# First mixture, state tokens: the tokens as loaded operand in both layers, summed in rows, turned once at the end

## The chip, the cores and the metric

One core of a Trainium2 chip runs the whole program. Its engines work beside each other, each through its own queue in order: TensorE (PE) multiplies 128x128 tiles into PSUM, VectorE (DVE), ScalarE (ACT) and GpSimd (POOL) work on vectors, and SyncE (SP) issues DMAs. A matmul instruction has two operands: one, of 128 columns, is loaded into the array ahead of it (a weight load, PEld in the profile), the other is streamed through it, with up to 512 columns. The metric is the device time of one execution in microseconds.

## The reference, cut to what matters

Attention between 4 x 512 tokens and 4 x 32 state tokens gives 2304 tokens of 512 features. A first mixture layer with a leaky activation follows, then a second mixture of 8 experts with a balanced gate.

```python
def _moe_ref(x, w_in, w_out, alpha):
    h = x @ w_in
    g = np.maximum(h, 0.0) + alpha * np.minimum(h, 0.0)
    return (g @ w_out).astype(np.float32)

def _moe2_ref(x, w_gate, w1, w2):
...
    for e in range(E):
        h = np.maximum(x @ w1[e], 0.0)
        ye = h @ w2[e]
        out += P[:, e:e + 1] * ye
```

In the first mixture `x` is 2304x512, `w_in` 512x2048 and `w_out` 2048x512. `P` comes from `exp` of the logits `x @ w_gate`, scaled eight times over its rows and columns.

## The kernel before

Matmuls are done in three terms: every operand is split into a high part and the rest of it (`wh_t`, `wl_t`; `xs[0]`, `xs[1]`; `gh`, `gl`), and low x high, high x high and high x low are summed in PSUM.

The first mixture goes through its 2048 hidden columns in 8 **units** `u` of `FU` = 256, each of `NF` = 2 halves `f` of 128. A unit has five **chunks** of tokens `c`: four of 512 tokens, and the last one, `c == CS`, the 128 **state tokens** (4 x 32). For a chunk there are two jobs: `layer1(u, c, f)` makes the hidden columns of half `f` and their activation, `layer2_first(u, c, d)` multiplies them by the unit's rows of `w_out` and gives one block `d` of 128 output features, which is added to `acc`. Everywhere the features stand in the partitions and the tokens in the columns, so that the weights are the loaded operand and the tokens are streamed: 512 columns for a normal chunk, 128 for the state chunk. (For normal chunks layer 1 has been rewritten: it streams attention weights against `v`, a product of state tokens and weights that `make_v` prepares for every unit in four pieces, each 6 matmuls of 256 columns, `pv`.)

The state chunk's layer 1 takes 4 feature tiles x 3 terms = 12 matmuls for each half, 24 in all; its layer 2 takes 2 halves x 3 terms for each of 4 blocks, again 24. All four blocks stand side by side in one PSUM bank and are added to `acc` at once.

After layer 1 come three steps: ACT takes the negative part out of PSUM (`r`, L527), DVE completes the leaky activation (`leak`, L530), ACT and POOL split it (`halves`, L535 and L536). They are not written down at once but put into a list `soon` with a number of **slots** to wait; `slot()` (L1236) is called after every half of layer 1 and every block of layer 2, runs what is due, and lets background work go one step: the lane `w` converts the next unit's weights from their loaded form (`to_f32`, L109 to L123: a chain over DVE, ACT, POOL and again DVE) and splits them (L138, L139), the lane `v` makes `v`, and near the end lanes make the experts' forms (L626 to L635) and the gate. So the number of slots decides where background work stands among the matmuls.

The jobs follow `order` (L1203): `program` puts layer 1 of the next chunk before layer 2 of the one before, so the state chunk's layer 2 comes after layer 1 of the next unit's chunk 0. Up to the first job of unit 2 a scheduler may reorder the instructions; from there on each engine runs them as written (`manual_schedule`). PSUM pools: `ps_h` (3 banks) for layer 1, `ps_o` (3) for layer 2, `ps_a` (2) for `pv`, transposes and the gate.

Of the kernel before, what the change touches and what calls it, by code (L numbers as in the profile page):

```python
# [8 lines left out]
F32 = mybir.dt.float32  # L9
# [35 lines left out]
def body(ctx: ExitStack, tc: tile.TileContext, xt_in, xn_in, stb, stk, wd, ws, alpha, wgate, out):  # L45
# [82 lines left out]
    def split_w(u, j):  # L128
# [8 lines left out]
        src = src_t[u, j]  # L137
        nc.scalar.activation(out=wh_t[u, j], in_=src, func=AF.Copy)  # L138
        nc.gpsimd.tensor_tensor(out=wl_t[u, j], in0=src, in1=f32(wh_t[u, j]), op=ALU.subtract)  # L139

    def w1(t, u, k, f):
        return t[u, f][:, k * P:(k + 1) * P]

    def w2(t, u, f, c0, n):
        return t[u, NF + f][:, c0:c0 + n]
# [355 lines left out]

    v_done = set()

    def layer1(u, c, f):
        n = S if c < CS else NS_ALL
        if f == 0:
            g_t[u, c] = (
                gp.tile([P, NF, S], F32R, tag="gh", name=f"gh{u}_{c}"),
                gp.tile([P, NF, S], F32R, tag="gl", name=f"gl{u}_{c}"),
            )  # L510
        gh, gl = g_t[u, c]
        ps = ps_h.tile([P, 512], F32, tag="h", name=f"ph{u}_{c}_{f}")[:, :n]
        if c < CS:
            vh, vl = (v_of(u, c)[i][:, :, f * P:(f + 1) * P] for i in range(2))
            terms = [(w[:, k, :], x[:, k, :]) for k in range(2) for w, x in ((vh, al[c]), (vh, ah[c]), (vl, ah[c]))]
        else:
            terms = [
                (w1(wt, u, k, f), x[:, k, :])
                for k in range(KD) for wt, x in ((wh_t, xs[1]), (wh_t, xs[0]), (wl_t, xs[0]))
            ]  # L520
        for i, (w, x) in enumerate(terms):
            nc.tensor.matmul(ps, lhsT=w, rhs=x, start=(i == 0), stop=(i == len(terms) - 1))  # L522
        hi, lo = gh[:, f, :n], gl[:, f, :n]
        fa = u * NF + f
        r = tp.tile([P, S], F32, tag="r", name=f"r{u}_{c}_{f}", bufs=3)[:, :n]

        nc.scalar.activation(out=r, in_=ps, func=AF.Relu, scale=-1.0)  # L527

        def leak():
            nc.vector.scalar_tensor_tensor(  # L530
                out=r, in0=r, scalar=beta[:, fa:fa + 1], in1=ps, op0=ALU.mult, op1=ALU.add
            )

        def halves():
            nc.scalar.activation(out=hi, in_=r, func=AF.Copy)  # L535
            nc.gpsimd.tensor_tensor(out=lo, in0=r, in1=f32(hi), op=ALU.subtract)  # L536

        soon.append([1, leak])
        soon.append([2, halves])

    def layer2_first(u, c, d):

        n = S if c < CS else NS_ALL
        gh, gl = g_t[u, c]
        if c < CS or d == 0:
            po_t[c < CS] = ps_o.tile([P, 512], F32, tag="o", name=f"po{u}_{c}_{d}")
        ps = po_t[c < CS][:, :n] if c < CS else po_t[False][:, d * n:(d + 1) * n]
        i = 0
        for f in range(NF):
            for wt, g in ((wh_t, gl), (wh_t, gh), (wl_t, gh)):  # L550
                nc.tensor.matmul(  # L551
                    ps, lhsT=w2(wt, u, f, d * P, P), rhs=g[:, f, :n], start=(i == 0), stop=(i == 3 * NF - 1)
                )
                i += 1
        bank = po_t[c < CS]

        def evict():
            for g, there, here in places(c):
                if g not in acc:
                    new_acc(g)  # L560
                if c < CS:
                    a, src = acc[g][:, d, there], bank[:, here]
                else:
                    a, src = acc[g][:, :, there], bank.rearrange("p (d n) -> p d n", d=KD)
                if u == 0:
                    nc.scalar.activation(out=a, in_=src, func=AF.Copy)
                else:
                    nc.vector.tensor_tensor(out=a, in0=src, in1=a, op=ALU.add)  # L568

        if c < CS or d == KD - 1:  # L570
            soon.insert(0, [1, evict])

    po_t = {}

# [659 lines left out]
    def slot():  # L1236
        tick()
        for lane in lanes:
            if wait[lane] > 0:
                wait[lane] -= 1  # L1240
            else:
                advance(lane)
# [96 lines left out]
    def run(program):  # L1339
        for kind, u, c in program:  # L1340
            if kind == 1:

                while done["a"] < min(c, B - 1):
                    advance("x")
                if c == CS:
                    states_to(B - 1)
                while (u, 1) not in split:
                    advance("w")
                while c < CS and u == 1 and done["scores"] < 2 + c // 2:
                    advance("x")  # L1350
                while c < CS and (u, c // 2) not in v_done:
                    advance("v")
                if (u, c) == (1, 2):
                    lanes["w"].append(convert(2, range(2)))
                if (u, c) == (2, 0):
                    nc.scalar.activation(out=wg[:, :, :E], in_=wg_raw, func=AF.Copy)
                    nc.vector.tensor_tensor(out=wg[:, :, E:], in0=wg_raw, in1=f32(wg[:, :, :E]), op=ALU.subtract)
                if (u, c) == (U1 - 1, 0):
                    while (u, NPIECE - 1) not in split:
                        advance("w")  # L1360
                    load_a(0, rawp)
                    lanes["w"].append(weights_a(0))
                if c == 0 and 2 <= u < U1 - 1:
                    lanes["w"].append(weights(u + 1, 0, 0 if u == U1 - 2 else 1))
                    lanes["v"].append(make_v(u + 1))
                for f in range(NF):
                    layer1(u, c, f)
                    slot()
                if (u, c) == (0, CS):

                    lanes["w"].append(weights(2, 2, 0))
                    lanes["v"].append(make_v(2))
            else:
                while (u, NPIECE - 1) not in split:
                    advance("w")
                if (u, c) == (0, 1):

                    states_to(1)
                    while (1, 2) not in split:
                        advance("w")  # L1380
                for i in range(KD):
                    layer2_first(u, c, i)
                    slot()
                if u == U1 - 1:

                    if c == 0:
                        made.update(forms(0))
                    forms_in(made, ("B11", "T1 T3 T2", "", "", "")[c])
                    if c == 2:
                        lanes["gate"].append(gate())  # L1390
                if u == U1 - 2 and c == 3:
                    forms_in(made, "B22")
                if (u, c) == (U1 - 1, CS):
                    forms_in(made, "B21 T4")
# [138 lines left out]
```

## Time and profile before

| | us |
|---|---|
| median of 3 runs (1855.04 to 1856.41) | 1856.17 |
| the profiled execution | 1851.04 |
| its span | 1849.3 |
| PE busy | 1781.9 (96%) |
| DVE, POOL, ACT busy | 1503.3, 1256.7, 732.4 |
| layer 1 of unit 2 begins | 174.5 |
| layer 1 of unit 6 begins | 344.9 |
| matmuls | 10163 |

The span is cut into three: about 145 us of attention mixed with units 0 and 1, then units in a period of 42.6 us up to some 345 us, then the last two units with the gate, and from about 440 us the experts. Busy PE is not PE at its peak: matmuls overlap, so what one costs in a row of matmuls is read from the distance of their starts, or from a row of the chain of waits divided by its count. A chain of waits follows back from the end: each step to what released it.

### The profile page before, as it was taken

How to read it: one execution, taken by the hardware profiler on the slowest of the kernel's cores; microseconds unless marked ns; L12 is line 12 of the kernel's file. 1: busy time of each engine (PE TensorE's matmuls, PEld its weight loads, DVE VectorE, ACT ScalarE, POOL GpSimd, SP SyncE). 2: the span in 40 equal slices, each digit the busy share in tenths (PEclk: the TensorE clock that was granted, in tenths of full speed). 3: DMA queues.
4: the chain of work that ended last, by engine and by line, in shares of the span. 5: the costliest groups of instructions: out<-in, count | busy, mean ns of one | idle time of the engine just before them, and what ended most of it. 6: DMA issues, size and time to landing. Idle time of an engine off the chain costs nothing.

```text
span 1849.3 us, 29270 instructions
## 1 busy us (share of the span) xinstructions
PE 1781.9 (96%) x10163; PEld 1659.5 (90%) x10163; DVE 1503.3 (81%) x2317; ACT 732.4 (40%) x1393; POOL 1256.7 (68%) x1297
## 2 busy tenths in 40 slices
PE   6799999998989999999999999999999999999998
PEld 5688788876878888898889999999999999999998
DVE  6744767776899999999997777777788888788777
ACT  6755666654334334443332222222223333332332
POOL 4523555555657778787757777777777898777775
PEclk8899999999999999999999999999999999999999
DMA  6111111121758899898797677777677778888884
GB/s 222 46 52 46 53 51 46 58 75 66 253 194 321 312 329 334 318 352 308 281 332 290 242 256 264 268 259 262 249 259 258 276 296 301 323 302 309 315 298 162
DMA packets 153010, 427.19 MB, mean 231 GB/s; under 512 B 17296, under 2 KB 34192, under 8 KB 152864
## 3 DMA queue, kind: packets, MB, share of 16 engines
q1 hardware_dynamic: 152864, 425.34, 63.7%
q8 instruction: 81, 1.33, 0.3%
q14 instruction: 65, 0.53, 0.1%
HBM read 302.28 MB, written 122.99 MB: 230 GB/s over the span
## 4 chain that ended last, share of the span: by engine, by line
PE 74%; DVE 13%; POOL 4%; issue 3%; ACT 3%; DMA 2%; SPq 0%; DVEq 0%; POOLq 0%; ACTq 0%
PE pm L1023 23%; PE py L850 12%; PE px L850 8%; PE pz L850 8%; PE po L551 8%; PE po L1168 7%; PE ph L522 4%; DVE oa L1190 2%; DVE wz L800 1%; DVE g2l L873 1%; POOL w2l L672 1%; PE pv L484 1%; DVE c L857 1%; DMA rw<-in_ws_dram 1%; PE psr L329 1%
## 5 line engine op out<-in xcount | busy, mean ns | idle before, releaser
L1029 DVE TENSOR_TENSOR m<-pm,m 128x768 f32<-128x768 f32 (+1 forms) x427 | 377.7, 886 | 124.6 <-PE pm L1023 124.6
L1023 PE MATMUL pm<-formgh,wz 128*128 128x384 f32 (+1 forms) x1134 | 212.6, 322 | 0.4 <-DVE m L1029 0.4
L954 POOL TENSOR_TENSOR formgh<-mid,formgh 128x384 fp32r<-128x384 f32 (+1 forms) x126 | 121.2, 962 | 107.0 <-ACT formgh L953 106.9
L850 PE MATMUL px<-rB,wah 128*128 128x384 f32 (+1 forms) x768 | 189.4, 329 | 3.4 <-DVE g2l L873 3.1
L850 PE MATMUL py<-rT,wsh 128*128 128x384 f32 (+1 forms) x768 | 188.1, 327 | 2.3 <-DVE u L857 2.3
L1023 PEld LDWEIGHTS pm<-formgh,wz 128*128 128x128 f32 x1134 | 186.7, 188 | 0.7 <-issue 0.7
L536 POOL TENSOR_TENSOR gl<-r,gh 128x512 fp32r<-128x512 f32 (+1 forms) x80 | 94.3, 1191 | 114.9 <-ACT gh L535 61.6
L872 ACT ACTIVATE g2h<-c 128x384 fp32r<-128x384 f32 x96 | 50.5, 526 | 301.5 <-DVE c L857 301.5
L672 POOL TENSOR_TENSOR w2l<-rw,w2h 128x512 fp32r<-128x512 f32 x64 | 87.5, 1388 | 121.2 <-ACT w2h L670 113.1
L1168 PE MATMUL po<-w2l,g2h 128*128 128x512 f32 x384 | 152.4, 397 | 0.0
L1168 PE MATMUL po<-w2h,g2h 128*128 128x512 f32 x384 | 151.6, 395 | 0.0
L1168 PE MATMUL po<-w2h,g2l 128*128 128x512 f32 x384 | 149.8, 390 | 0.0
L850 PEld LDWEIGHTS px<-rB,wah 128*128 128x128 f32 x768 | 135.9, 188 | 11.7 <-DVE g2l L873 6.1
L850 PEld LDWEIGHTS py<-rT,wsh 128*128 128x128 f32 x768 | 135.9, 188 | 5.7 <-DVE u L857 2.7
L964 POOL TENSOR_TENSOR T<-mid,mid 128x384 f32<-128x384 f32 (+1 forms) x126 | 118.2, 961 | 30.8 <-DVE mid L938 29.5
L953 ACT ACTIVATE formgh<-mid 128x384 fp32r<-128x384 f32 (+1 forms) x126 | 63.0, 500 | 178.9 <-DVE mid L938 137.3
L551 PE MATMUL po<-gl,wh 128*128 128x512 f32 (+1 forms) x320 | 120.1, 376 | 13.0 <-DVE acc L568 11.3
L1190 DVE SCALAR_TENSOR_TENSOR oa<-po,pr,oa 128x512 f32<-128x512 f32 x168 | 124.3, 740 | 8.1 <-PE po L1168 7.4
L938 DVE SCALAR_TENSOR_TENSOR mid<-mid,pb 128x384 f32<-128x384 f32 (+1 forms) x192 | 123.1, 641 | 6.6
L850 PE MATMUL px<-rB,wal 128*128 128x384 f32 (+1 forms) x384 | 125.5, 327 | 0.0
L850 PE MATMUL py<-rT,wsl 128*128 128x384 f32 (+1 forms) x384 | 125.3, 326 | 0.0
L1023 PE MATMUL pm<-formgl,w2h 128*128 128x384 f32 (+1 forms) x504 | 121.1, 323 | 2.8 <-DVE m L1029 1.8
(260 smaller groups left out, 5156.7 us busy)
## 6 DMA issues: line engine op xcount, KB each, us to landing
wz<-kept_bs SPq DMA_DIRECT2D x126, 512.0 KB, 8.1
kept_bs<-wz SPq DMA_DIRECT2D x64, 512.0 KB, 6.2
wsh<-kept_as_h SPq DMA_DIRECT2D x64, 512.0 KB, 3.7
wsl<-kept_as_l SPq DMA_DIRECT2D x64, 512.0 KB, 6.0
wah<-kept_a_h SPq DMA_DIRECT2D x64, 384.0 KB, 2.9
wal<-kept_a_l SPq DMA_DIRECT2D x64, 384.0 KB, 4.3
w2h<-kept_b_h SPq DMA_DIRECT2D x63, 384.0 KB, 6.5
w2l<-kept_b_l SPq DMA_DIRECT2D x63, 384.0 KB, 7.2
```

The lines of the kernel that those rows point to most:

```text
L522: nc.tensor.matmul(ps, lhsT=w, rhs=x, start=(i == 0), stop=(i == len(terms) - 1))
L536: nc.gpsimd.tensor_tensor(out=lo, in0=r, in1=f32(hi), op=ALU.subtract)
L551: nc.tensor.matmul(ps, lhsT=w2(wt, u, f, d * P, P), rhs=g[:, f, :n], start=(i == 0), stop=(i == 3 * NF - 1))
L672: nc.gpsimd.tensor_tensor(out=lo[:, i], in0=src[:, i], in1=f32(hi[:, i]), op=ALU.subtract)
L850: nc.tensor.matmul(bank[b], lhsT=w[:, k * P:(k + 1) * P], rhs=xf[:, j, k, :], start=(first and i == 0), stop=(i == 5), skip_group_check=True,)
L938: nc.vector.scalar_tensor_tensor(out=out, in0=src, scalar=0.0, in1=pb[:, e % 2, h * n:(h + 1) * n], op0=ALU.max, op1=ALU.mult)
L954: nc.gpsimd.tensor_tensor(out=lo, in0=out, in1=f32(hi), op=ALU.subtract)
L964: nc.gpsimd.tensor_tensor(out=out, in0=x, in1=y, op=ALU.subtract)
L1023: nc.tensor.matmul(ps[:, q, :n], lhsT=w[:, q * P:(q + 1) * P], rhs=x, start=(j == 0), stop=(j == 2))
L1029: nc.vector.tensor_tensor(out=mm[g][name], in0=ps[:, :, :n], in1=mm[g][name], op=ALU.add)
L1168: nc.tensor.matmul(ps, lhsT=x[:, f, t * P:(t + 1) * P], rhs=w[:, f, :], start=(i == 0), stop=(i == 3 * NF - 1))
L1190: nc.vector.scalar_tensor_tensor(out=a, in0=ps, scalar=p, in1=a, op0=ALU.mult, op1=ALU.add)
```

## The change

For the state chunk, the tokens (`xs`) become the loaded operand and the weights are streamed: `layer1_state` makes both halves at once with 12 matmuls of 256 columns, with the state tokens in the partitions ("rows"). ACT copies them out of PSUM, and two slots later PE turns them (`turn`, two transposes), after which the activation goes on as before, for both halves at once. `layer1(u, CS, 1)` does nothing, its slot stays. Layer 2 loads the activations and streams the 512 output features, 6 matmuls, called for `NF` = 2 halves in place of 4 blocks, so it has two slots in place of four. The sum in `acc` keeps the tokens in the partitions through all units; after the last unit `turn_state` turns it with four transposes and ACT copies it back.

```diff
@@ -137,9 +137,6 @@
         src = src_t[u, j]
         nc.scalar.activation(out=wh_t[u, j], in_=src, func=AF.Copy)
         nc.gpsimd.tensor_tensor(out=wl_t[u, j], in0=src, in1=f32(wh_t[u, j]), op=ALU.subtract)
-
-    def w1(t, u, k, f):
-        return t[u, f][:, k * P:(k + 1) * P]
 
     def w2(t, u, f, c0, n):
         return t[u, NF + f][:, c0:c0 + n]
@@ -501,8 +498,56 @@
 
     v_done = set()
 
+    def layer1_state(u):
+
+        gh, gl = g_t[u, CS] = (
+            gp.tile([P, NF, S], F32R, tag="gh", name=f"gh{u}_{CS}"),
+            gp.tile([P, NF, S], F32R, tag="gl", name=f"gl{u}_{CS}"),
+        )
+        ps = ps_h.tile([P, 512], F32, tag="h", name=f"pr{u}")[:, :FU]
+        terms = [
+            (x[:, k, :], w[u][:, :, k * P:(k + 1) * P])
+            for k in range(KD) for w, x in ((wh_t, xs[1]), (wh_t, xs[0]), (wl_t, xs[0]))
+        ]
+        for i, (x, w) in enumerate(terms):
+            nc.tensor.matmul(
+                ps.rearrange("p (f c) -> p f c", f=NF), lhsT=x, rhs=w, start=(i == 0), stop=(i == len(terms) - 1)
+            )
+        rows = tp.tile([P, S], F32, tag="r", name=f"rows{u}", bufs=3)[:, :FU]
+        nc.scalar.activation(out=rows, in_=ps, func=AF.Copy)
+
+        def turn():
+            ph = ps_h.tile([P, 512], F32, tag="h", name=f"ph{u}_{CS}")[:, :FU]
+            for f in range(NF):
+                nc.tensor.transpose(ph[:, f * P:(f + 1) * P], rows[:, f * P:(f + 1) * P], ident)
+            r = tp.tile([P, S], F32, tag="r", name=f"r{u}_{CS}", bufs=3)[:, :FU]
+            nc.scalar.activation(out=r, in_=ph, func=AF.Relu, scale=-1.0)
+
+            def leak():
+                for f in range(NF):
+                    fa = u * NF + f
+                    at = slice(f * P, (f + 1) * P)
+                    nc.vector.scalar_tensor_tensor(
+                        out=r[:, at], in0=r[:, at], scalar=beta[:, fa:fa + 1], in1=ph[:, at], op0=ALU.mult, op1=ALU.add
+                    )
+
+            def halves():
+                r2 = r.rearrange("p (f n) -> p f n", f=NF)
+                hi, lo = gh[:, :, :NS_ALL], gl[:, :, :NS_ALL]
+                nc.scalar.activation(out=hi, in_=r2, func=AF.Copy)
+                nc.gpsimd.tensor_tensor(out=lo, in0=r2, in1=f32(hi), op=ALU.subtract)
+
+            soon.append([1, leak])
+            soon.append([2, halves])
+
+        soon.append([2, turn])
+
     def layer1(u, c, f):
-        n = S if c < CS else NS_ALL
+        if c == CS:
+            if f == 0:
+                layer1_state(u)
+            return
+        n = S
         if f == 0:
             g_t[u, c] = (
                 gp.tile([P, NF, S], F32R, tag="gh", name=f"gh{u}_{c}"),
@@ -510,14 +555,8 @@
             )
         gh, gl = g_t[u, c]
         ps = ps_h.tile([P, 512], F32, tag="h", name=f"ph{u}_{c}_{f}")[:, :n]
-        if c < CS:
-            vh, vl = (v_of(u, c)[i][:, :, f * P:(f + 1) * P] for i in range(2))
-            terms = [(w[:, k, :], x[:, k, :]) for k in range(2) for w, x in ((vh, al[c]), (vh, ah[c]), (vl, ah[c]))]
-        else:
-            terms = [
-                (w1(wt, u, k, f), x[:, k, :])
-                for k in range(KD) for wt, x in ((wh_t, xs[1]), (wh_t, xs[0]), (wl_t, xs[0]))
-            ]
+        vh, vl = (v_of(u, c)[i][:, :, f * P:(f + 1) * P] for i in range(2))
+        terms = [(w[:, k, :], x[:, k, :]) for k in range(2) for w, x in ((vh, al[c]), (vh, ah[c]), (vl, ah[c]))]
         for i, (w, x) in enumerate(terms):
             nc.tensor.matmul(ps, lhsT=w, rhs=x, start=(i == 0), stop=(i == len(terms) - 1))
         hi, lo = gh[:, f, :n], gl[:, f, :n]
@@ -540,19 +579,19 @@
 
     def layer2_first(u, c, d):
 
-        n = S if c < CS else NS_ALL
         gh, gl = g_t[u, c]
         if c < CS or d == 0:
             po_t[c < CS] = ps_o.tile([P, 512], F32, tag="o", name=f"po{u}_{c}_{d}")
-        ps = po_t[c < CS][:, :n] if c < CS else po_t[False][:, d * n:(d + 1) * n]
-        i = 0
-        for f in range(NF):
-            for wt, g in ((wh_t, gl), (wh_t, gh), (wl_t, gh)):
-                nc.tensor.matmul(
-                    ps, lhsT=w2(wt, u, f, d * P, P), rhs=g[:, f, :n], start=(i == 0), stop=(i == 3 * NF - 1)
-                )
-                i += 1
         bank = po_t[c < CS]
+        if c < CS:
+            terms = [
+                (w2(wt, u, f, d * P, P), g[:, f, :]) for f in range(NF) for wt, g in ((wh_t, gl), (wh_t, gh), (wl_t, gh))
+            ]
+        else:
+            terms = [(g[:, d, :NS_ALL], w2(wt, u, d, 0, DM)) for wt, g in ((wh_t, gl), (wh_t, gh), (wl_t, gh))]
+        for i, (w, x) in enumerate(terms):
+            first_of, last_of = (c < CS or d == 0) and i == 0, (c < CS or d == NF - 1) and i == len(terms) - 1
+            nc.tensor.matmul(bank, lhsT=w, rhs=x, start=first_of, stop=last_of)
 
         def evict():
             for g, there, here in places(c):
@@ -567,10 +606,18 @@
                 else:
                     nc.vector.tensor_tensor(out=a, in0=src, in1=a, op=ALU.add)
 
-        if c < CS or d == KD - 1:
+        if c < CS or d == NF - 1:
             soon.insert(0, [1, evict])
 
     po_t = {}
+
+    def turn_state():
+        (g, there, _), = places(CS)
+        a = acc[g][:, :, there]
+        ps = ps_a.tile([P, KD, NS_ALL], F32, tag="a", name="pts")
+        for d in range(KD):
+            nc.tensor.transpose(ps[:, d, :], a[:, d, :], ident)
+        nc.scalar.activation(out=a, in_=ps, func=AF.Copy)
 
 
 
@@ -1378,9 +1425,11 @@
                     states_to(1)
                     while (1, 2) not in split:
                         advance("w")
-                for i in range(KD):
+                for i in range(KD if c < CS else NF):
                     layer2_first(u, c, i)
                     slot()
+                if (u, c) == (U1 - 1, CS):
+                    soon.append([3, turn_state])
                 if u == U1 - 1:
 
                     if c == 0:
```

The order of each engine from unit 2 on changes; here are two places (line numbers of after are those of the changed kernel). **DVE at the start of unit 4**, before. `raw_0` and `y_0` are the weight conversion (L115 is its middle step, L123 its last, fed by POOL), `r_1_0` and `r_1_1` the leaks of chunk 1, `acc<-po_4_0` the addition of the state chunk of unit 3:

```order
L109 TENSOR_SCALAR y_0_2394<-raw_0_2120 128x512
L530 SCALAR_TENSOR_TENSOR r_0_1_2391<-r_0_1_2391,beta,ph_0_1_2384 128x512
L115 SCALAR_TENSOR_TENSOR raw_0_2120<-raw_0_2120 128x512
L123 SCALAR_TENSOR_TENSOR raw_0_2120<-raw_0_2120 128x512
L568 TENSOR_TENSOR acc_1342<-po_4_0_2398,acc_1342 128x4x128
L530 SCALAR_TENSOR_TENSOR r_1_0_2442<-r_1_0_2442,beta,ph_1_0_2435 128x512
L109 TENSOR_SCALAR y_1_2461<-raw_1_2217 128x512
L530 SCALAR_TENSOR_TENSOR r_1_1_2458<-r_1_1_2458,beta,ph_1_1_2451 128x512
L568 TENSOR_TENSOR acc_679<-po_0_0_2465,acc_679 128x512
```

and in the changed kernel:

```order
L109 TENSOR_SCALAR y_0_2292<-raw_0_2050 128x512
L569 SCALAR_TENSOR_TENSOR r_0_1_2289<-r_0_1_2289,beta,ph_0_1_2282 128x512
L115 SCALAR_TENSOR_TENSOR raw_0_2050<-raw_0_2050 128x512
L607 TENSOR_TENSOR acc_1328<-po_4_0_2296,acc_1328 128x4x128
L569 SCALAR_TENSOR_TENSOR r_1_0_2321<-r_1_0_2321,beta,ph_1_0_2314 128x512
L123 SCALAR_TENSOR_TENSOR raw_0_2050<-raw_0_2050 128x512
L569 SCALAR_TENSOR_TENSOR r_1_1_2331<-r_1_1_2331,beta,ph_1_1_2324 128x512
L607 TENSOR_TENSOR acc_679<-po_0_0_2335,acc_679 128x512
```

The conversion's last step on `raw_0` has moved behind the state chunk's addition and the first leak of chunk 1, and `y_1`, the next piece's first step, behind the first addition of chunk 0.

**ACT at the end of unit 4**, before. `y_3` is the conversion's last piece, `v<-pv` are the copies of the v product, `r_4_0` and `r_4_1` take the two halves of the state chunk, `gh_4` splits them:

```order
L119 ACTIVATE y_3_2631<-y_3_2631,full 128x512
L120 ACTIVATE y_3_2631<-y_3_2631 128x512
L494 ACTIVATE v_790<-pv_1_1_2678 64x512
L494 ACTIVATE v_789<-pv_1_1_2678 64x512
L527 ACTIVATE r_4_0_2713<-ph_4_0_2700 128x128
L138 ACTIVATE wh_2_2613<-raw_3_2449 128x512
L527 ACTIVATE r_4_1_2733<-ph_4_1_2720 128x128
L535 ACTIVATE gh_4_2698<-r_4_0_2713 128x128
L535 ACTIVATE gh_4_2698<-r_4_1_2733 128x128
```

and in the changed kernel, where `rows<-pr` is the copy that the turn waits for:

```order
L491 ACTIVATE v_789<-pv_1_0_2543 64x512
L491 ACTIVATE v_790<-pv_1_0_2543 64x512
L119 ACTIVATE y_3_2531<-y_3_2531,full 128x512
L120 ACTIVATE y_3_2531<-y_3_2531 128x512
L517 ACTIVATE rows_2581<-pr_2568 128x256
L491 ACTIVATE v_790<-pv_1_1_2584 64x512
L491 ACTIVATE v_789<-pv_1_1_2584 64x512
L524 ACTIVATE r_4_2606<-ph_4_2603 128x256
L138 ACTIVATE wh_2_2513<-raw_3_2349 128x512
L537 ACTIVATE gh_4_2566<-r_4_2606 128x2x128
```

The copy of the rows stands behind the two copies of `pv_1_0` and the last two steps on `y_3`, and ahead of the copies of `pv_1_1`, which before came ahead of the state chunk.

On PE there are, between the last state matmul and the turn, the six matmuls of `pv_1_1` and the six of block `po_3_0`.

## Rows read from the trace of the kernel before

**Rows 1.** The page, part 1: busy us, share of span, instructions

```profile
PE 1781.9 (96%) x10163; PEld 1659.5 (90%) x10163; DVE 1503.3 (81%) x2317; ACT 732.4 (40%) x1393; POOL 1256.7 (68%) x1297
```

**Rows 2.** Stretches (start:end, length): engines, granted clock, DMA; columns first

```profile
core 0: us, PE busy (x) PEld busy (x) DVE busy (x) ACT busy (x) POOL busy (x), PEclk, DMA share, GB/s
162.00:164.40 2.40, 0.00 (x0) 0.01 (x1) 1.48 (x3) 2.33 (x5) 1.10 (x1) 1.00 0.00 0
166.00:169.30 3.30, 3.30 (x12) 2.82 (x12) 1.68 (x3) 1.77 (x5) 1.84 (x3) 0.50 0.49 155
259.60:302.20 42.60, 41.38 (x218) 35.14 (x217) 31.05 (x51) 27.07 (x48) 22.12 (x18) 1.00 0.15 49
480.00:1849.00 1369.00, 1347.72 (x7781) 1290.04 (x7779) 1180.89 (x1776) 446.04 (x864) 1019.52 (x1081) 1.00 0.78 284
```

**Rows 3.** Chain of waits through unit 4: start and length in us, what

```profile
251.43 2.63 PE ph L522 x24
...
262.33 2.42 PE po L551 x22
...
266.10 1.29 POOL gl L536
267.39 1.27 POOL raw L121
...
269.29 0.69 DVE acc L568
...
277.50 4.08 PE po L551 x18
281.58 0.71 PE pv L484 x6
```

**Rows 4.** Timeline of PE: start, length, what, idle before and releaser

```profile
273.09 0.50 PE L551 MATMUL po<-gl,wh 128*128 128x512 f32 x1 [1.22 <-DVE acc L568]
```

**Rows 5.** Timeline of DVE, same place

```profile
268.69 0.69 DVE L123 SCALAR_TENSOR_TENSOR raw<-raw 128x512 int32<-128x512 int32 x1 [4.28 <-POOL raw L121]
```

**Rows 6.** Chain of waits: a transpose, units 0 to 2, begin of unit 6

```profile
86.78 1.09 PE pst L295 x8
...
145.69 2.53 PE ph L522 x23
...
148.24 0.68 ACT wh L138
...
164.42 0.95 PE pv L484 x6
165.37 1.89 PE ph L522 x12
167.25 2.43 PE po L551 x6
...
174.50 2.72 PE ph L522 x12
...
344.88 2.72 PE ph L522 x12
```

**Rows 7.** Timeline of ACT, end of unit 4

```profile
293.64 0.63 ACT L120 ACTIVATE y<-y 128x512 int32<-128x512 f32 x1
```

**Rows 8.** Chain of waits in the last two units

```profile
391.85 5.06 PE po L551 x21
...
405.12 0.76 DVE acc L568 x2
...
410.19 3.42 DVE rT L635 x4
...
419.84 0.61 DVE acc L568
```

**Rows 9.** Waits from 355 to 470 us: who for whom, us, times, longest

```profile
PE po L551 <- DVE acc L568: 6.5, 4, 3.2
...
PE po L551 <- POOL gl L536: 1.7, 3, 0.9
```

## The prediction, as it stood before the changed kernel ran

> **What bounds the kernel now.** I read the page's busy shares first: TensorE (PE) is busy 96% of the span, VectorE (DVE) 81% [rows 1]. Then the table by stretches [rows 2]: in a steady unit of the first mixture (42.6 us) PE is busy 41.4 us, while DVE has 31.1 us, ScalarE (ACT) 27.1 us and GpSimd (POOL) 22.1 us of work; the long stretch behind it, the experts from 480 us on, is PE-bound and untouched. So time taken from PE in the first mixture counts, as long as the other engines, which run in a fixed order, don't come late instead. Where they do now is seen in the chain of waits of one unit [rows 3]: PE all through, but for one piece from 264.8 to 273.1 us that goes over POOL and DVE. The timelines show what that is: PE stands 1.22 us for an accumulation on DVE [rows 4], and DVE had itself stood 4.28 us in front of the weight conversion's last step, whose input POOL makes [rows 5].
>
> **What the matmuls cost.** A unit's state chunk is 24 narrow matmuls in each layer, eight units in all. Layer 1 takes 2.63 us for 24, layer 2 2.42 us for 22: 110 ns apart, however narrow they are. A matmul with 512 loaded columns takes 4.08/18 = 227 ns, one with 256 0.71/6 = 118 ns [rows 3]. So after the change layer 1 is 12 x 118 ns = 1.42 us (1.21 less) and layer 2 is 6 x 227 ns = 1.36 us (1.28 less). Added: two turns of 128x128; eight such transposes took 1.09 us [rows 6], 136 ns each, so 0.27 us. Net on PE 2.2 us a unit, 8 units: 17.8 us; the four turns at the very end (0.55 us) go off that, and stand where PE waits for DVE anyway.
>
> The rows price a narrow matmul at 110 ns, as if something other than its 128 columns set it. The Trainium skill, "TensorE: Matmul & The Clock Gate", section "Back-to-back issue gap", gives 134 cycles (56 ns) for 128 columns and 216 ns for 512: by that formula the old 24 cost 1.34 us, the new six 1.30 us, and the change loses its turns. Its section "LDWEIGHTS" prices loading a 128-column operand at 107 ns, and the trace agrees with that one (110 ns measured).
>
> **The other engines.** ACT: one 256-wide copy of the rows more, but one 256-wide Relu and one 256-wide rounding instead of two 128-wide ones each; about even. POOL: one subtraction for two. DVE: the same two leaks and one accumulation. Queues and loads stand as before. Hidden cost: PE now waits for ACT in the middle of the chunk, since the turn needs the copied rows. PE has a v product (0.71) and an output block (1.36) between them, 2.1 us of cover. In the trace ACT works there without a gap: the conversion's last ACT step there ends at 294.27 [rows 7], when PE has just begun the state chunk. In the new order the two v copies, that step and then the rows' copy (0.4, between the 128-wide and the 512-wide ACT steps) come after each other. Laid out with the trace's durations the rows are there some 1.7 us before PE gets to the turn; behind the turn stand three output blocks and the next layer 1 (6.8 us) before layer 2 needs its result. I take 0; if the cover were gone, each us of it would be paid eight times.
>
> **A steady unit.** Two slots fewer in layer 2 also move the weight conversion against PE: the DVE order shown with the change has the blocked step two places later, behind the state accumulation and one leak. I lay the piece from 262.2 us out again. PE: layer 2 of the state chunk to 263.5, layer 1 of chunk 1 to 266.3, the first half of the next block to 267.0. There it waits for POOL, whose second subtraction ends at 266.10 + 1.29 = 267.4 as before [rows 3]: 0.5 us. Blocks end at 268.2, 269.5, 270.9. The fourth needs the first one's bank: POOL's conversion ends at 268.66 [rows 3], then DVE does the blocked step, a leak and that accumulation, some 0.7 us each [rows 3, 5], to 270.7: in time. So the fourth block starts at 270.9 in place of 273.09 [rows 4], 2.2 us earlier. With layer 1 (1.21) less the turns (0.27) a unit gains 3.1 us. Bounds: 0.94 if all that layer 2 frees turns into waiting, 2.2 if the old wait stays, 3.6 with no wait at all. I take 3.1, since every row in the layout is one that the change leaves alone. Four units lie between 174.5 and 344.9 us, where layer 1 of units 2 and 6 begins [rows 6]: **12.4 us** (8.9 to 14.4).
>
> **The start.** At 148.24 ACT begins to split new weights into the buffer that layer 1 of the first state chunk was reading; POOL, a load, the conversion, a leak and the v copies hang on it, and PE stands from 162.0 to 164.4 [rows 2, 6]. That layer 1 ends 1.2 us sooner, so this chain comes 1.2 us sooner; the work that waits at its end changes (an output block's second half in place of a v product), and I lay its release out at 162.2. Behind it PE had 10.1 us up to 174.5; now it has half a block, the turn, two v products and three blocks, 6.5 us at their prices, since the second state chunk's layer 1 has moved ahead of the wait. So unit 2 begins at 168.7, 5.8 us earlier. In the trace the clock falls after the wait, to 0.50 of full, the 1.2 GHz level, from 166.0 to 169.3 [rows 2]: 12 state matmuls in 1.89 us, an output block in 2.43 [rows 6], together 1.6 us over their prices. If the shorter wait still brings that, the gain is 4.2, and some 1 us less if the release comes with the old wait's length. I take **4.5 us** (3 to 5.8).
>
> **The last two units.** Up to 391.85, where PE waits for POOL [rows 8], lie one unit's piece as above (2.2), one layer 1 with turns (0.94) and one layer 2 (1.28): 4.4 us. PE stands there four more times behind the last weights' conversion, some 3 us in all (of the waits from 355 us on, 6.5 us for DVE and 1.7 for POOL, the two named elsewhere here, 1.2 and 3.2, and one of 0.9 behind them left out [rows 9]); in the new order that conversion has no v copies between its steps. I take 4.9 (2 if POOL's chain doesn't move, 7.3 if no wait is left). Then one more layer 1 with turns, 0.94. From 405.12 to 419.84 DVE is never idle, and the accumulation that starts then ends PE's longest wait, 3.2 us [rows 8, 9]: the last layer 2's 1.28 us lie under it and gain nothing by themselves. But with two slots fewer, two of the expert forms' steps (0.8 us for one of four in 3.42 us, 0.6 the other) come behind the accumulation that PE waits for: 1.4 us (0 to 1.4). Together **7.2 us** (3 to 9).
>
> **The sum.** 12.4 + 4.5 + 7.2 = 24.1 us. The profiled execution took 1851.04 us, 1849.3 of it span: 1826.9 by its own time. The median of the runs is 1856.17, 5.1 us above it; I take the difference over to the median: 1856.2 - 24.1 = 1832 us.
>
> **The rivals.**
> 1. *The freed time turns into other waits.* DVE has 31.1 us in what would be 39.5, 79%, in a fixed order, and DVE and POOL already set the waits [rows 3, 5, 9]. For it: every wait that PE has there is for one of them; against: the blocked step moves to where its input is nearly ready, and nowhere else in the unit does PE wait. If in the units only layer 1 counts and the ends give their low values: 4 x 0.94 + 3 + 3 = 9.8, and with half of the rest some 14 us: 1842 to 1846.
> 2. *The turn comes late (slower).* In each unit PE stands before the turn because ACT's copy of the rows is behind conversion steps that wait for DVE. Price: 8 x lateness beyond the 1.7 us that I find. The gain of 24.1 is gone at 3.0 us a unit; at 3.5 us the kernel is 4 us slower, 1860 us. For it: ACT is dense there; against: the steps ahead of the copy are short and ready.
> 3. *Narrow matmuls weren't dear.* If a matmul cost its columns only, 227/4 = 57 ns for 128, the old 24 would be 1.36 us, the new 1.42 and 1.36, and the turns a loss: 8 x 0.33 = 2.6 us slower, 1859. Against it: 24 in 2.63 us with PE never idle [rows 3]. This is what the cited gap rule would give.
> 4. *The end of the first mixture doesn't carry over*, since DVE's forms or loads hold the experts' start: only a few us, 1853 to 1856. Against: the experts' loads and buffers are released by steps that move along.
>
> **How the numbers follow.** My forecast (20 to 29 us gained) 0.58; more than that 0.04; rival 1 (4 to 20 us) 0.30; no change, by rival 4 or by all of it hidden, 0.04; slower, by rivals 2 and 3, 0.04. About 0.2%, 3.7 us, is what a measurement of this kernel can tell from no change. So faster 0.92, same 0.04, slower 0.04. The range: the high ends of the three terms give 14.4 + 5.8 + 9 = 29.2 us, 1827; the low ones 8.9 + 3 + 3 = 14.9, 1841, and one us more takes in enough of rival 1: 1827 to 1842.
>
> **What would show it.** In the new profile the steady unit is about 39.5 us long; layer 1 of the state chunk is 12 matmuls in 1.4 us, layer 2 six in 1.36; PE's wait for an accumulation is gone from the units, and a wait of about 0.5 us for POOL's subtraction stands there; PE does not wait before the turn; layer 1 of unit 2 starts near 169 us, and the experts' products some 24 us sooner. Wrong would be: idle PE in front of the turn with ACT's copy as releaser (rival 2), units of 41 us with DVE as releaser (rival 1), or a pitch of the wide matmuls well over 118 and 227 ns.

## The result, and the profile after

The changed kernel takes 1838.62 us (median of 4, 1838.12 to 1841.0) against 1855.61 for the one before: a ratio of 0.9911, 95% interval 0.9894 to 0.9928, or 17.0 us less. Two repeats gave 0.9897 [0.9876, 0.9918] and 0.9911 [0.9894, 0.9929]. The forecast was 1832 us in a range of 1827 to 1842, 24.1 us less: the direction and the range hold, and some 30% of the forecast gain is missing.

The page of the changed kernel, part 1, answers to [rows 1]. PE lost 11.7 us of busy time, DVE gained 12.9, though its instructions are as many as before:

```profile
PE 1770.2 (96%) x9943; PEld 1639.4 (89%) x9943; DVE 1516.2 (83%) x2317; ACT 736.0 (40%) x1386; POOL 1252.6 (68%) x1289
```

Whole times are a blunt measure here. In twelve profiles the first matmul of unit 0's state chunk begins anywhere from 145.2 to 150.8 us, and the experts behind the first mixture take 1393 to 1401 us. (The two profiles of the kernel before have 1393.9 and 1394.5 there, the three of the changed one 1395.7 to 1397.5; since the changed kernel with four slots, below, has 1393.2 and one with half of the change 1400.6, I call that variation, but no run shows where it comes from.) The time from that matmul to the experts agrees among repeats within 0.6 us. So the first mixture is measured by itself, in three pieces, whose ends are read from the timeline of PE in each kernel: **start** (first state matmul of unit 0 to layer 1 of unit 2), **units** 2 to 5 (to layer 1 of unit 6), **end** (to the experts' `px` matmul with 0.16 to 0.18 us of idle time ahead of it). Times in us; the kernels behind the first two are those of the experiments.

| kernel | start | unit 2 | unit 4 | units 2 to 5 | end | sum |
|---|---|---|---|---|---|---|
| before | 28.81 | 42.52 | 42.63 | 170.39 | 110.04 | 309.24 |
| after | 22.91 | 42.97 | 40.56 | 164.61 | 103.60 | 291.12 |
| layer 1 alone | 24.87 | 42.29 | 42.37 | 169.49 | 108.17 | 302.53 |
| layer 2 alone | 24.12 | 42.51 | 41.21 | 166.51 | 109.01 | 299.64 |
| after, four slots | 23.02 | 41.39 | 41.32 | 165.38 | 107.38 | 295.78 |
| after, split later | 23.06 | 42.97 | 39.58 | 161.74 | 103.15 | 287.95 |
| the same, low term last | 22.47 | 42.97 | 39.47 | 161.40 | 104.95 | 288.82 |
| split later, unit 2 mended | 23.19 | 39.57 | 39.61 | 158.39 | 103.31 | 284.89 |
| the same, unit 6 too | 22.95 | 39.60 | 39.60 | 158.42 | 103.71 | 285.08 |

The change gains 18.1 us in the sum: 5.9 in the start (forecast 4.5), 5.8 in the units (12.4), 6.4 in the end (7.2).

**A steady unit.** Unit 4 of the changed kernel, in the columns of [rows 2]: 40.56 us. PE's busy time fell from 41.38 to 39.62 us, and DVE's work rose from 31.05 to 32.51 us:

```profile
core 0: us, PE busy (x) PEld busy (x) DVE busy (x) ACT busy (x) POOL busy (x), PEclk, DMA share, GB/s
254.15:294.71 40.56, 39.62 (x189) 32.33 (x188) 32.51 (x52) 27.59 (x48) 22.40 (x17) 1.00 0.17 52
```

Its chain of waits, and the turn as it stands in the last unit's chain (start, length, what):

```profile
263.33 0.04 DVE raw L123
263.37 1.65 issue
265.01 0.73 DVE r L569
265.75 0.61 DVE acc L607
266.36 0.04 issue
266.40 1.66 PE po L594 x6
...
286.62 1.43 PE pr L513 x12
...
293.21 1.66 PE po L594 x6
...
388.73 0.22 PE ph L522 x2
```

Layer 1 of the state chunk is 12 matmuls in 1.43 us (forecast 1.42), the turn costs 0.22 (0.27). What is new is at the top: the conversion's last step L123, one instruction of DVE, and 1.65 us in which it waits for nothing that the profile shows. The timelines of the place (PE, DVE, POOL; in brackets idle time before and its releaser) answer to [rows 4, 5]:

```profile
256.87 0.39 PE L594 MATMUL po<-wh,gl 128*128 128x512 f32 x1
...
262.09 0.50 PE L594 MATMUL po<-gl,wh 128*128 128x512 f32 x1 [0.28 <-POOL gl L575]
...
265.41 0.39 PE L594 MATMUL po<-gh,wl 128*128 128x512 f32 x1
266.40 0.50 PE L594 MATMUL po<-gl,wh 128*128 128x512 f32 x1 [0.60 <-DVE acc L607]
266.74 0.40 PE L594 MATMUL po<-gh,wh 128*128 128x512 f32 x1
```

```profile
263.33 1.76 DVE L123 SCALAR_TENSOR_TENSOR raw<-raw 128x512 int32<-128x512 int32 x1 [0.91 <-POOL raw L121]
265.01 0.73 DVE L569 SCALAR_TENSOR_TENSOR r<-r,beta,ph 128x512 f32<-128x512 f32 x1
265.67 0.68 DVE L607 TENSOR_TENSOR acc<-po,acc 128x512 f32<-128x512 f32 x1
```

```profile
261.99 1.31 POOL L121 TENSOR_TENSOR raw<-y,raw 128x512 int32<-128x512 int32 x1
263.25 1.29 POOL L575 TENSOR_TENSOR gl<-r,gh 128x512 fp32r<-128x512 f32 x1
265.87 1.31 POOL L139 TENSOR_TENSOR wl<-raw,wh 128x512 fp32r<-128x512 f32 x1 [1.33 <-ACT wh L138]
```

L123 takes 1.76 us where it took 0.69 [rows 5]. POOL's subtraction `gl_1` began 0.08 us ahead of it and ends at 264.54, and L123 ends 0.55 us after that. In the kernel before, POOL stood still there: its next instruction was `wl_0`, which needs L123's result. PE pays at the fourth block, 266.40: the pitch of such matmuls is 0.23 us, the two around the stop start 0.99 and 0.34 us apart, so 0.60 us shown as idle are 0.87 us lost.

### The profile page after: what moved, and what is told of

It is laid out like the page before. It is cut to its first block, busy times and chain, and to the rows that moved or that the text cites. A ratio compares the mean times of both kernels' runs of the same rounds, so it can differ in the third digit from the quotient of the medians.

```text
span 1836.3 us, 28786 instructions
## 1 busy us (share of the span) xinstructions
PE 1770.2 (96%) x9943; PEld 1639.4 (89%) x9943; DVE 1516.2 (83%) x2317; ACT 736.0 (40%) x1386; POOL 1252.6 (68%) x1289
## 3 DMA queue, kind: packets, MB, share of 16 engines
q8 instruction: 80, 1.31, 0.3%
## 4 chain that ended last, share of the span: by engine, by line
PE 70%; DVE 17%; issue 4%; ACT 3%; POOL 3%; DMA 2%; SPq 0%; DVEq 0%; POOLq 0%; ACTq 0%
PE pm L1070 23%; PE py L897 12%; PE px L897 8%; PE pz L897 8%; PE po L1215 6%; PE po L594 6%; PE ph L561 3%; DVE oa L1237 2%; DVE wz L847 2%; DVE g2l L920 1%; DVE c L904 1%; DVE sumb L740 1%; DMA kept_bs<-wz 1%; DVE sumb L743 1%; DVE u L904 1%
## 5 line engine op out<-in xcount | busy, mean ns | idle before, releaser
L897 PEld LDWEIGHTS px<-rB,wah 128*128 128x128 f32 x768 | 135.7, 188 | 11.7 <-DVE g2l L920 6.1
L575 POOL TENSOR_TENSOR gl<-r,gh 128x512 fp32r<-128x512 f32 x64 | 87.6, 1377 | 76.9 <-ACT gh L574 58.2
L1011 POOL TENSOR_TENSOR formgh<-T,formgh 128x384 fp32r<-128x384 f32 (+1 forms) x126 | 121.9, 967 | 0.0
```

What stands on the lines that cost most here:

```text
L897: nc.tensor.matmul(bank[b], lhsT=w[:, k * P:(k + 1) * P], rhs=xf[:, j, k, :], start=(first and i == 0), stop=(i == 5), skip_group_check=True,)
L1011: nc.gpsimd.tensor_tensor(out=out, in0=x, in1=y, op=ALU.subtract)
```

## The experiments

**The same kernels again**, to see which differences are the change's. Before:

> The kernel before once more, for a second profile. If the differences between the two profiles in stretches that the change doesn't touch (attention up to 130 us, where after is 2.2 us later, and the experts from 480 us on, where it is 2.9 us longer) are variation from run to run, they change here by as much; if they belong to the change, this profile agrees with the first of before within 0.5 us in both stretches. Layer 1 of units 2 and 6 170.4 us apart (174.5 to 344.9), DVE's last conversion step (L123) 0.69 us at the median.

The first stretch moved: layer 1 of unit 2 begins at 177.12 in place of 174.34 us. The experts' stretch did not (1393.9 us). The three pieces were 28.96, 170.4 and 110.5 us, the sum 309.8. After:

> The changed kernel once more. Theory (the gain fell short because the conversion's last step on DVE, L123, takes 1.76 us in place of 0.69 while POOL's subtraction gl_1 runs beside it): in units 3 to 6 that step is again 1.7 to 1.8 us, a unit 40.5 us, 1838 to 1840 us in all. Rival (chance of that one profile): L123 0.7 us in most units and a unit near 39.5 us.

1837.83 us (1836.14 to 1839.91), the pieces 22.94, 164.64 and 103.59. L123 took 1.77 us in units 3 to 6 at the same four places, each within 0.2 us. A third time, beside the last but one kernel below:

> The changed kernel once more, beside the one before on the same chip. 1836 to 1840 us, units 3 to 5 of 40.55 us, unit 2 of 42.9 us. If the kernel with both mended orders is really faster, it is 4 to 7 us below this one (3.1 us in units 3 to 5 and the piece of unit 6, 2 to 3 us in unit 2).

1837.35 us (1834.96 to 1840.91), units of 40.6, unit 2 of 42.95. The slow L123 is no accident of one profile.

**Each half alone.** Layer 1 with the tokens loaded, layer 2 as it was; and the other way round:

```diff
 # layer 1 alone: layer2_first, its loop and evict as before, no turn_state
-                for i in range(KD if c < CS else NF):
+                for i in range(KD):
 # layer 2 alone: layer1 as before, no layer1_state
-        if c == CS:
-            if f == 0:
-                layer1_state(u)
-            return
```

> Only layer 1 with the tokens loaded, and the turn; layer 2 in four blocks and four slots as before, no turn at the end. By PE's own times a unit gains 1.21 - 0.27 = 0.94 us (eight units 7.5 us), and the 1.22 us wait for DVE stays, since the conversion doesn't move against PE: units of 41.7 us, 1847 to 1849 us, some 7 to 9 us under before. Rival (freed time turns to waits): units of 42.3 us or more, under 4 us gained. Rival (the turn comes late): idle PE before the two transposes, no gain.

> Only layer 2 with the activations loaded, in two slots, with the turn after the last unit; layer 1 as before. By PE's own times a unit gains 1.28 us, and the conversion's last step moves behind the state accumulation, which saves up to 0.9 us of the old wait: units of 40.4 to 41.3 us, 1843 to 1847 us. If the slow L123 (1.76 us) comes with the two slots, it is seen here too, with about 0.6 us of wait for an accumulation in a unit. Rival (what layer 2 frees turns into waits): units of 42.3 us, 1851 us or more. If the two parts simply add, this gain and that of layer 1 alone make the 17 us of both.

Layer 1 alone: 1849.93 us (1845.36 to 1851.2), ratio 0.9954 [0.9938, 0.9971], which is 8.5 us less (5.4 to 11.5). The gain in all is the theory's, but the unit is the rival's: 42.37 us, a gain of 0.26 in place of 0.94, since the old stop stays and a new one comes behind the state chunk:

```profile
269.06 0.50 PE L590 MATMUL po<-gl,wh 128*128 128x512 f32 x1 [1.16 <-DVE acc L607]
...
291.74 0.47 PE L590 MATMUL po<-gl,wh 128*128 128x512 f32 x1 [0.30 <-DVE acc L607]
```

Most of its gain, 3.9 of 6.7 us in the sum, is in the start. Layer 2 alone: 1845.38 us, 0.9928 [0.9904, 0.9951], units of 41.21, as the theory had it. L123 is slow here too, and PE stops twice:

```profile
267.60 1.75 DVE L123 SCALAR_TENSOR_TENSOR raw<-raw 128x512 int32<-128x512 int32 x1 [0.92 <-POOL raw L121]
```

```profile
266.35 0.51 PE L555 MATMUL po<-gl,wh 128*128 128x512 f32 x1 [0.29 <-POOL gl L536]
...
270.67 0.50 PE L555 MATMUL po<-gl,wh 128*128 128x512 f32 x1 [0.62 <-DVE acc L568]
```

In the kernel with layer 1 alone L123 took 0.70 us at 264.66. So the slow step came with layer 2's two slots, not with the rows or the turn. By the sums the halves give 6.7 + 9.6 = 16.3 us, both together 18.1.

**Two slots or four.** The changed kernel with four slots for the state chunk's layer 2, from unit 1 on:

```diff
                 for i in range(KD if c < CS else NF):
                     layer2_first(u, c, i)
                     slot()
+                    if c == CS and u:
+                        slot()
```

> The changed kernel, but the state chunk's layer 2 counts four slots again in place of two (from unit 1 on), so that the weight conversion keeps its old place among the matmuls; the matmuls are those of the change. Theory (the slot shift earns as much as the cheaper matmuls of layer 2): L123 is back at 0.69 us, but the conversion is late again, PE stands some 1.2 to 2.4 us for the accumulation in front of the fourth block, units of 41.1 to 42.3 us in place of 40.55, 1841 to 1847 us. Rival (the shift is worth nothing or costs, since it brings the slow L123): units of 40.5 us or less, 1836 to 1839 us.

1841.22 us, 0.9918 [0.99, 0.9935], at the low end of the theory's range; units of 41.32. L123 takes 0.69, with DVE standing 3.67 us for its input, and PE stops three times:

```profile
264.10 0.50 PE L594 MATMUL po<-gl,wh 128*128 128x512 f32 x1 [0.27 <-POOL gl L575]
...
268.66 0.50 PE L594 MATMUL po<-gl,wh 128*128 128x512 f32 x1 [0.89 <-DVE acc L607]
...
291.37 0.47 PE L594 MATMUL po<-gl,wh 128*128 128x512 f32 x1 [0.34 <-DVE acc L607]
```

So of the cheaper matmuls alone (2.25 us a unit) the units keep 1.31; the shift of the conversion is worth 0.76 us more a unit even with the slow L123. In the end the two slots are worth 3.8 us (103.60 against 107.38). In unit 2, though, the four slots are better, 41.39 against 42.97.

**POOL's order at L123.** The split of chunk 1's first half one slot later, so that POOL has `wl_0` ahead of `gl_1` again; and with it the term that needs POOL's low half put last in the second half of a block:

```diff
-        soon.append([2, halves])
+        soon.append([3 if (c, f) == (1, 0) else 2, halves])
 # and, in the second kernel only
-  (w2(wt, u, f, d * P, P), g[:, f, :]) for f in range(NF) for wt, g in ((wh_t, gl), (wh_t, gh), (wl_t, gh))
+  (w2(wt, u, f, d * P, P), g[:, f, :]) for f in range(NF)
+  for wt, g in (((wh_t, gh), (wl_t, gh), (wh_t, gl)) if f else ((wh_t, gl), (wh_t, gh), (wl_t, gh)))
```

> The changed kernel, but the split of the first half of chunk 1 (ACT's gh, POOL's gl_1) is put down one slot later, so that POOL has the weights' subtraction wl_0 in front of gl_1, as in the kernel before, and stands still while DVE does the conversion's last step on the first piece. Theory (L123 takes 1.76 us in place of 0.69 because POOL subtracts beside it): L123 takes 0.69 us in every unit, the stop of PE in front of the fourth block (0.60 us idle, 0.87 with what it costs around it) is gone, units of 39.7 us, 1833 to 1836 us. Rival (it is the new place itself, behind a leak, or the wait for POOL that makes it slow): L123 stays at 1.76 us, units of 40.55 us, 1837 to 1840 us.

> As the one before, and in layer 2 of the normal chunks the term with the low part of the second half of the hidden columns comes last of six in place of fourth, so that PE needs POOL's second subtraction two matmuls (0.46 us) later. Theory (the 0.28 us of idle time for POOL in each unit, 0.55 with what it costs around it, is the wait that the prediction put at 0.5): it is gone, another 0.3 to 0.55 us a unit, 1830 to 1834 us. Rival (the freed time turns into a stop for the accumulation at the fourth block): the same time as the one before within 1 us.

With the later split that L123 took 0.69 us in units 3 to 6, behind the same POOL step and the same wait of 0.9 us as in the changed kernel; only POOL's next instruction differs, and comes 1.5 us later:

```profile
259.98 0.69 DVE L123 SCALAR_TENSOR_TENSOR raw<-raw 128x512 int32<-128x512 int32 x1 [0.90 <-POOL raw L121]
```

```profile
258.65 1.30 POOL L121 TENSOR_TENSOR raw<-y,raw 128x512 int32<-128x512 int32 x1
261.46 1.32 POOL L139 TENSOR_TENSOR wl<-raw,wh 128x512 fp32r<-128x512 f32 x1 [1.51 <-ACT wh L138]
```

The stop at the fourth block is gone, the unit takes 39.58 us. The total, 1835.57 us, 0.9891 [0.9871, 0.991], can't be told from that of the changed kernel by itself; the sum of the pieces is 3.2 us less. The low term last removes the stop for `gl` (none is left in units 3 to 5), but the unit falls by 0.11 us and not by 0.55: the fourth block now starts the moment that DVE's accumulation is through (260.91 + 0.68 = 261.59 us). That stop shows 0.01 us of idle time and costs 0.29: from the last matmul of the third block (the first of the two in the row) to the second of the fourth it is 0.74 us in place of 0.45. The rest goes in delays under 0.1 us each:

```profile
261.25 0.90 PE L595 MATMUL po<-gl,wh 128*128 128x512 f32 x2
261.99 0.40 PE L595 MATMUL po<-gh,wh 128*128 128x512 f32 x1
```

The end grows by 1.8 us: its stops for accumulations are 2.83 and 2.41 us in place of 1.41 and 0.87. The rival held: 1835.8 us, the same.

**Unit 2**, which had gained nothing. Its rows in the changed kernel, PE and DVE:

```profile
179.04 0.50 PE L594 MATMUL po<-gl,wh 128*128 128x512 f32 x1 [0.75 <-POOL gl L575]
183.23 0.50 PE L594 MATMUL po<-gl,wh 128*128 128x512 f32 x1 [0.49 <-DVE acc L607]
192.21 0.47 PE L594 MATMUL po<-gl,wh 128*128 128x512 f32 x1 [0.53 <-DVE acc L607]
212.13 0.50 PE L594 MATMUL po<-gl,wh 128*128 128x512 f32 x1 [1.09 <-DVE acc L607]
```

```profile
180.80 1.77 DVE L123 SCALAR_TENSOR_TENSOR raw<-raw 128x512 int32<-128x512 int32 x1 [0.15 <-POOL raw L121]
...
189.64 1.76 DVE L123 SCALAR_TENSOR_TENSOR raw<-raw 128x512 int32<-128x512 int32 x1 [0.16 <-POOL raw L121]
...
200.19 1.18 DVE L123 SCALAR_TENSOR_TENSOR raw<-raw 128x512 int32<-128x512 int32 x1
```

On the kernel with the later split:

```diff
                 if (u, c) == (2, 0):
+                    flush("w")
```

> The kernel with the later split of chunk 1, and in unit 2 the weight conversion begins one slot earlier (what is left of the one before is written down at once in front of layer 1 of unit 2), so that DVE, ACT and POOL have the same order there as in units 3 to 6. Theory (unit 2 gained nothing because two slots fewer in the state chunks of units 0 and 1 start its conversion one slot late, so that three of its last steps run beside POOL's subtractions, 1.76, 1.76 and 1.18 us, and PE stops for accumulations three times, 0.49, 0.53 and 1.09 us): those L123 take 0.69 us, the three stops are gone or under 0.3 us, unit 2 takes 39.6 to 40.7 us in place of 42.9, and the total is 2 to 3 us under the kernel with the later split, 1831 to 1834 us. Rival (unit 2 is long because PE enters it late, behind the start's wait): the stops stay, unit 2 takes 42 us or more.

The three L123 took 0.69 us each, the stops for accumulations are gone, and unit 2 takes 39.57 us. The total, a little below the range that I expected, is 1830.04 us (1826.94 to 1832.98), 0.987 [0.9849, 0.989] of before and 7.3 us below the changed kernel in the same comparison, whose interval (0.9911 [0.9894, 0.9929]) it overlaps nowhere. PE's waits from 165 to 340 us (who for whom, us, times, longest), in the changed kernel:

```profile
PE po L594 <- DVE acc L607: 4.0, 6, 1.1
PE po L594 <- POOL gl L575: 1.6, 4, 0.7
```

and with both orders mended:

```profile
PE po L594 <- POOL gl L575: 1.3, 5, 0.3
```

In the kernel before it was 4.8 us in 4 stops, all for an accumulation.

**The same step in the end.** In unit 6 an L123 took 1.81 us beside POOL's `gl_2`, and PE stood 1.83 us for `v`. On the last kernel:

```diff
-        soon.append([3 if (c, f) == (1, 0) else 2, halves])
+        soon.append([3 if (c, f) == (1, 0) or (u, c, f) == (U1 - 2, 2, 0) else 2, halves])
```

> The kernel with both mended orders, and the same later split for chunk 2 of unit 6, where DVE's L123 again took 1.81 us beside POOL's gl_2 and PE then stood 1.83 us for DVE's rest of v. Theory (POOL's subtraction, and nothing of the place, holds L123): that L123 takes 0.69 us, PE's stop for v falls by 1.1 us to some 0.7, and the end of the first mixture is up to 1.1 us shorter, as far as the accumulation that PE waits for next (1.41 us) doesn't take it back; 1828 to 1832 us in all. Rival (this L123 is slow for another reason): it stays at 1.8 us and the stop at 1.83.

L123 took 0.69 us and the stop for `v` 0.72, as the theory had it; and with it went the fall of the clock that had come behind that stop (granted 0.50 from 358.80 to 362.20 us before this edit, 1.00 from 360.30 to 363.70 with it): PE was 2.6 us ahead. But the next stop, for an accumulation, grew from 1.41 to 2.74 us, and now the clock fell behind that one, to 0.51 from 372.20 to 375.60. The two took all of it back. The end is 103.71 us, the total 1831.33 us, 0.9861 [0.984, 0.9882]: no gain over the kernel before it. The cause was right, and mending this place alone gained nothing.

## Why the prediction was right, and where it fell short

- **What bounds the kernel, and the prices of the matmuls: right.** PE's work in a unit fell by what the rows said. Six wide matmuls of layer 2 take 1.36 us (256.87 to the next matmul at 258.23), 12 of layer 1 1.43, the turn 0.22. Before, the 24 narrow ones of either layer took 2.63: 2.25 us net, forecast 2.2. (The columns that the prediction calls loaded in its prices of 227 and 118 ns are the streamed ones.) So narrow matmuls did cost their 110 ns, and rival 3, that they weren't dear, is out, with the 57 ns apiece that would have made it true.
- **The turn: right.** PE shows no idle time ahead of it in any profile. The rows' copy ends at 289.21 and the turn starts at 290.00: 0.8 us of cover, not the 1.7 that I laid out, but enough. Rival 2 is out.
- **The start: 5.9 us, forecast 4.5** (3 to 5.8). The sum without the fall of the clock, 5.8, was the one that came, and its parts with it: the wait ends 16.3 us behind the first state matmul (laid out at 16.7), and 6.6 us of work lie behind it (6.5). PE waits 1.37 us at 162.71 in place of 2.4, and from 164.10 to 167.40 the granted clock is 1.00, the 2.4 GHz level, where before it was 0.50 from 166.0 to 169.3 [rows 2]. Of the two possibilities I had given the wrong one more weight.
- **The end: 6.4 us, forecast 7.2** (3 to 9). The sum holds, its terms don't, and that they cancel is luck. Up to the matmul that stood at 391.85 I had 4.9 us, at least 2. Counted from the begin of unit 6, it comes 1.4 us sooner. Of the four old stops behind the conversion, 3.0 us, only one is left, of 1.36 us, but PE now stands for `v` in unit 6, where it didn't before, and behind that the granted clock falls to 0.50, the 1.2 GHz level (columns as in [rows 2]):

```profile
362.46 0.50 PE L561 MATMUL ph<-al,v 128*128 128x512 f32 x1 [0.59 <-ACT v L491]
365.03 0.50 PE L561 MATMUL ph<-ah,v 128*128 128x512 f32 x1 [1.83 <-DVE v L494]
366.60:369.90 3.30, 3.30 (x10) 2.66 (x10) 0.49 (x1) 2.06 (x3) 1.10 (x1) 0.50 0.02 5
```

The step that failed here is that the conversion, with no v copies between its steps, would no longer hold PE. The last pieces of `v` stood on DVE behind an L123 of 1.81 us and a leak instead; with that L123 mended the stop of 1.83 is 0.72. The cheaper layer 1 and layer 2 that follow and the long stop, 3.15 us before and 0.86 now, bring the lead to 5.2 us. Some 1.5 more, which no term of mine had, came from the clock: before, it fell behind the long stop, and in the changed kernel it didn't (a row of each):

```profile
421.90:425.30 3.40, 3.40 (x10) 2.62 (x9) 1.74 (x4) 0.34 (x1) 0.00 (x0) 0.50 0.02 5
405.80:409.10 3.30, 3.24 (x14) 2.70 (x15) 3.30 (x7) 0.12 (x1) 0.54 (x1) 1.00 0.00 0
```

So this piece holds least well of the three against being touched: time freed there turned into another stop twice (the low term last, unit 6 mended), and a stop that moves can take a stretch at half the clock with it.

- **The steady unit: 3.1 us forecast, 2.07 measured, and in unit 2 a loss of 0.45.** This is the main step that failed: 4 x 3.1 = 12.4 became 5.8. The layout held up to one duration. "DVE does the blocked step, a leak and that accumulation, some 0.7 us each" had 0.69 for L123 from the row where POOL stood still [rows 5], and took as ground that every row in the layout is one that the change leaves alone. The instruction was left alone, what POOL does beside it wasn't: I had compared the orders of DVE and ACT and not that of POOL, where the shift by two slots put `gl_1` right behind `raw_0`. L123 took 1.76, the fourth block stopped for 0.60 us in place of being in time, 0.87 us with what a stop costs around it. With POOL's order put back and all else left, the unit is 39.58 us; I had forecast 39.5, with a stop for POOL's subtraction of 0.5 us, where 0.28 shown and 0.55 lost were found.
- **Unit 2 is not like the others: missed.** I multiplied a unit's piece by four. The same two slots, missing in the state chunks of units 0 and 1, also start unit 2's conversion one slot late (its first L123 comes 10.2 us after the unit's begin, in units 3 to 5 9.2, with the order mended 9.1); there two of its steps L123 stood wholly behind subtractions of POOL and a third in part. That is 42.97 - 39.57 = 3.4 us.
- **The sum.** Those 3.4 us in unit 2 and 1.0 in each of units 3 to 5 make up most of the 6.6 us by which the units fell short of 12.4 (mended, the four take 158.39 us in place of 164.61, 6.2 less); the start's 1.4 more and the end's 0.8 less nearly cancel. With both orders mended the same matmuls gain 24.4 us in the sum of the pieces and 24.1 us by the ratio (20.4 to 28.0), as the forecast had it for a kernel that wasn't the one that ran: 5.6, 12.0 and 6.7 us in the three pieces, for 4.5, 12.4 and 7.2. The agreement of the sum within 0.3 us is better than that of its terms.
- **Rival 1** (freed time turns into waits) got 0.30 and holds in part: with layer 1 alone a unit kept 0.26 of 0.94 us, with four slots 1.31 of 2.25, and in the end mending one stop only made the next one longer and moved the fall of the clock behind it. Units of 41 us with DVE as releaser, its mark, lie between the 40.56 measured and the 41.32 with four slots. Rival 4 is out: the experts begin 18 us sooner on the pieces' clock.

## What to carry to other kernels

A duration taken from a trace holds for the instruction and for what the other engines do beside it: before it goes into a layout, look at the slowest of its group too, and at what ran there. When an edit changes how many slots or steps a stage has, compare the order of every engine, the idle one too, and in the first and last rounds apart. When an edit frees time on the busiest engine, moving the work that ends its next wait can be worth as much as the edit.

## What the hardware showed that I had not expected

A DVE instruction with both inputs in SBUF (L123) stands until POOL's subtraction is through, if POOL began first. The rows of unit 4 give 0.08 us of head start and an end 0.55 us after POOL's; in unit 2, caught halfway, it took 1.18 us. ACT stood still meanwhile in unit 4, so its half of the split is not what holds L123. The twelve profiles have 384 L123. All 125 that took more than 0.72 us have an instruction of POOL that began ahead of them, and they end 0.54 to 0.56 us after its end. Of the 259 others 12 have one, and it ends within 0.12 us of their begin. DVE's leaks and accumulations, which read one operand from PSUM, keep their 0.67 to 0.75 us beside the same POOL instructions. The kernel before had it in its trace, in the line of all L123 (count, then min/median/max in ns), and I took the median:

```profile
L123 DVE SCALAR_TENSOR_TENSOR raw<-raw x29: 675/694/1776, 16.3 to 381.5; 128x512 int32<-128x512 int32 x29
```

The Trainium skill, "SBUF — State Buffer", section "Who interferes with whom", states it: a DVE instruction with two SBUF inputs contends with a GpSimd instruction that reads SBUF, since its second input comes through the read interface that the two engines share, and the shared pair of ports is an exclusive lock. The trace agrees, 1.76 us against 0.69.

POOL pays the other way round: two subtractions in a row took 2.99 us beside L123 in unit 2, and 2.55 where no such instruction of DVE ran beside them. No experiment was made for that side, but the traces show it: the 95 subtractions of 128x512 that began during an L123 took 1.75 us at the median and ended 1.15 us after it, the 100 that began ahead of one took 1.29.
